# Softmax sums taken once per pair of heads, and two weight operations of VectorE moved to the other half of the pair

## The chip, the cores and the metric

One core of one Trainium2 chip. The metric is the device time of one execution in microseconds (us). The kernel before takes 1670.32 us, the median of 3 runs (1670.14 to 1671.12).

## What is computed

Attention with queries pooled in twos, and behind it a feed-forward layer with tanhshrink:

```python
q_pool = q.reshape(B, H, S // 2, 2, D).mean(axis=3)          # B, H, S, D = 8, 8, 1152, 64
scores = np.matmul(q_pool, k.transpose(0, 1, 3, 2)) / np.sqrt(D)
attn = np.exp(scores - scores.max(-1, keepdims=True))
attn = attn / (attn.sum(-1, keepdims=True) + 1e-09)
x = np.matmul(attn, v)              # to 4608 tokens of 512
h = x @ w_in                        # 512 to 2048
out = (h - np.tanh(h)) @ w_out      # 2048 to 512
```

The product with v is taken with the exponentials as they are. The sums of the exponentials are found beside it, and the division by them comes later, when x is read again.

## The kernel before

**Attention** works on 32 pairs of heads (8 batches of 4 pairs). A pair has 576 pooled queries and 1152 keys, and both heads of a pair lie on the 128 partitions, 64 each. Time is written out by hand in units: a pair has U = 36 units, a half of the queries (HQ = 288) has G = 18, and in every second unit the loop at the end computes one tile of scores of 128 keys (`scores`: eight matmuls, then an exponential of ScalarE into a tile `p_f`). All other work is hung on units by `add(u, f)`, and `run` calls what hangs on a unit, in the order in which it was added. `InOrder` keeps every engine to this order. What the units say is only an order: an engine goes on as soon as the waits of its next instruction are over.

In the same units as the scores of one pair, the next pair is prepared: its operands are split into a high and a low part (`hi_part`, `lo_part`), and the maxima of its scores are found. `max_part` is a matmul of 384 columns for both heads into a double bank of PSUM named `ps`, and in the unit behind it VectorE reduces it into `mx`. There are four double banks in all (`ps_a`), used in turn by scores, maxima, the transpose of the maxima (`turn`) and the products with v. `max_rows`, in the last unit of a first half, makes the maxima of all parts into rows (`nm`, `turn`, `mt`).

At the end of each half (unit 17 of the half) stands `pv`: the product of the nine `p_f` tiles of this half with v, and right behind it `z_sums`, the products of the sums of p with a tile of ones, for the half **before** this one (`late`). The sums over most keys are made by GpSimd (`z_part`: five additions per half into three tiles `z`, of keys 0 to 2, 3 to 5, and 6 and 7); the ninth tile of p goes into the product as it is. In `z_sums` four groups of 32 PSUM partitions are used: heads in steps of 32, tiles in steps of 64, so that each sum comes out in two parts, which `reciprocals` adds.

ScalarE takes both results out of PSUM (`o_out`, `z_out`), the store goes to DRAM once per pair, and once per batch the sums are read back in four DMAs (`sums`), 11 units later VectorE takes the reciprocals (`reciprocals`, two instructions on 128x36), and `spread` writes them for later use.

**Weights** of the feed-forward layer are converted in 32 blocks during attention (`w_block`), one per pair. Offsets count from a unit 5 of a pair. The table of operations gives five operations of VectorE at +48, which is unit 17 of a pair, the end of its first half: clamp, sign, shift, exponent, low part. GpSimd adds at +50 and subtracts at +68, ScalarE converts at +12 and +66.

```python
            for i, op in ((12, begin),
                          (48, lambda: ts(whole(t[0]), whole(t[0]), -top, top, op0=ALU.max, op1=ALU.min)),
                          (48, lambda: ts(t[1], t[0], -0x80000000, None, op0=ALU.bitwise_and)),
                          (48, lambda: stt(t[1], t[0], 3, t[1], op0=ALU.logical_shift_left, op1=ALU.bitwise_or)),
```

**Feed-forward** runs over nine chunks of tokens from line 506 on; its order is set by a scheduler that works from the program.

Of the kernel before, what the change touches and what calls it, by code (L numbers as in the profile page):

```python
# [43 lines left out]
def kernel(  # L44
# [40 lines left out]


    x_dram = dram.tile([NP, P, NTOK], F32, name="x_dram")
    z_dram = dram.tile([B, 2, 2, NP, SQ], F32, name="z_dram")
    r_dram = dram.tile([B, 2, NP, SQ], F32, name="r_dram")
    m_dram = dram.tile([2, 2, 2 * (5 * P + 64)], F32, name="m_dram")  # L90
    wi_dram = dram.tile([NF, P, 2, NP, P], F32, name="wi_dram")
    wo_dram = dram.tile([NF, P, 2, DM], F32, name="wo_dram")
# [1 line left out]
    def load_x(tiles, raw, sp, mul, hi, t0, n):  # L94

        x_h, x_l = (t.rearrange("p (c n) -> p c n", c=NP) for t in tiles())

        t = {}

        def fetch(hp):  # L100
            x, r = t[hp] = raw(hp)
            sp.dma_start(x[:, 0:n], x_dram[hp, :, t0:t0 + n])
            c = t0
            while c < t0 + n:
                b, c1 = divmod(c, SQ)
                m = min(SQ - c1, t0 + n - c)
                for h in range(2):
                    sp.dma_start(r[h * 64:h * 64 + 64, c - t0:c - t0 + m],
                                 r_dram[b, h, hp:hp + 1, c1:c1 + m].broadcast_to([64, m]))
                c += m  # L110

        def divide(hp):
            x, r = t[hp]
            mul.tensor_tensor(x[:, 0:n], x[:, 0:n], r[:, 0:n], op=ALU.mult)  # L114

        def hi_part(hp):
            hi(x_h[:, hp, 0:n], t[hp][0][:, 0:n])

        def lo_part(hp):
            mul.tensor_tensor(x_l[:, hp, 0:n], t[hp][0][:, 0:n], x_h[:, hp, 0:n].bitcast(F32), op=ALU.subtract)  # L120
        return x_h, x_l, [[lambda hp=hp, f=f: f(hp) for f in (fetch, divide, hi_part, lo_part)] for hp in range(NP)]
# [18 lines left out]
    with ExitStack() as actx:  # L140
# [47 lines left out]
        def load(pi):  # L188
            w = pairs[pi] = Pair()
            w.b, w.hp = divmod(pi, NP)  # L190
            w.i = pi % 2
            w.mb = mb[w.i]
            w.q_n = ld.tile([P, 2, SQ], F32, name="q_n")
            w.kq = ld.tile([P, KQ], F32, name="kq")
            sp.dma_start(w.q_n, q[w.b, w.hp])
            sp.dma_start(w.kq[:, SQ:], k[w.b, w.hp])
# [101 lines left out]
        class Half:  # L298
            pass

        late = []

        def z_part(hf, kts):

            z = zp.tile([P, 2, HQ], F32, name="z")
# [5 lines left out]
        def pv(u, hf):  # L311

            w, ps = hf.w, banks()
            hf.o = ps[:, 0]
            for kt in range(KT):
                for h in range(2):
                    pe.matmul(hf.o[64 * h:64 * h + 64, 0:HQ], w.v[:, h, kt], hf.p[kt][:, h], start=(kt == 0),
                              stop=(kt == KT - 1), tile_position=(0, 64 * h))
            add(u + 1, o_out, w, hf, at=first)
            if late:  # L320
                z_sums(u, late.pop(), ps[:, 1])
            late.append(hf)

        def z_sums(u, hf, ps):

            for g, z in enumerate(hf.zs + hf.p[-1:]):
                for h in range(2):
                    r = 64 * (g % 2) + 32 * h
                    pe.matmul(ps[r:r + 32, 0:HQ], ones, z[:, h], start=(g < 2), stop=(g > 1), tile_position=(0, r))
            add(u + 1, z_out, u + 1, hf.w, hf, ps, at=first)  # L330

        def o_out(w, hf):
            if hf.n == 0:
                w.o_s = sm.tile([P, SQ], F32, name="o_s")
                w.z_s = sm.tile([P, SQ], F32, name="z_s")
            act.activation(w.o_s[:, hf.n * HQ:(hf.n + 1) * HQ], hf.o[:, 0:HQ], AF.Copy)

        def z_out(u, w, hf, ps):

            act.activation(w.z_s[:, hf.n * HQ:(hf.n + 1) * HQ], ps[:, 0:HQ], AF.Copy)  # L340
            if hf.n == 1:
                def store():
                    sp.dma_start(x_dram[w.hp, :, w.b * SQ:(w.b + 1) * SQ], w.o_s)
                    sp.dma_start(z_dram[w.b].rearrange("r h a s -> (r h) a s")[:, w.hp], w.z_s[0:P:32])
                add(u + 2, store)
                if w.hp == NP - 1:
                    add(u + 6, lambda: tot.append((w.b, sums(w.b))))
                    if w.b < B - 1:
                        add(u + 17, lambda: reciprocals(dve, *tot[0]))
                        add(u + 20, lambda: spread(sp, *tot.pop(0)))  # L350

        def sums(b):

            n = NP * 2 * SQ // P
            t = rec.tile([P, 2, n], F32, name="rec")
            for r in range(2):
                for h in range(2):
                    sp.dma_start(t[h * 64:h * 64 + 64, r], z_dram[b, r, h].rearrange("a (x n) -> (a x) n", n=n))
            return t

        def reciprocals(eng, b, t):

            eng.scalar_tensor_tensor(t[:, 0], t[:, 0], 1e-9, t[:, 1], op0=ALU.add, op1=ALU.add)
            eng.reciprocal(t[:, 0], t[:, 0])

        def spread(dma, b, t):
            dma.dma_start(r_dram[b].rearrange("h a (x n) -> (h a x) n", n=SQ * NP * 2 // P), t[:, 0])

        WB = 512

        def w_block(u, kind, r, c):

            top = float.fromhex("0x1.dffffep-96")
            raw = wp.tile([P, WB, 2], I32, name="w_raw", bufs=3)
            lo, hi = raw.bitcast(mybir.dt.uint16)[:, :, 1], raw[:, :, 1]
            ts, stt = dve.tensor_scalar, dve.scalar_tensor_tensor
            t = []

            def begin():

                t[:] = [wp.tile([P, WB], I32, name=f"w_{i}", bufs=1 + (i < 2)) for i in range(3)]
                t.append(wp.tile([P, 2, WB], F32R, name="w_hl", bufs=2))
                act.activation(whole(t[0]), whole(hi), AF.Copy, scale=2.0 ** -112)

            def whole(x):
                return x.bitcast(F32)

            def store():
                src = t[3].bitcast(F32)
                if kind == 0:  # L390
                    f = c // P
                    sp.dma_start(wi_dram[f:f + WB // P, :, :, r].rearrange("f p s m -> p s f m"),
                                 src.rearrange("p s (f m) -> p s f m", m=P))
                else:
                    sp.dma_start(wo_dram[r, :, :, c:c + WB], src)
            sp.dma_start(raw.rearrange("p n w -> p (n w)"),
                         (w_in, w_out)[kind][r * P:(r + 1) * P, 2 * c:2 * (c + WB)])
            for i, op in ((12, begin),
                          (48, lambda: ts(whole(t[0]), whole(t[0]), -top, top, op0=ALU.max, op1=ALU.min)),
                          (48, lambda: ts(t[1], t[0], -0x80000000, None, op0=ALU.bitwise_and)),  # L400
                          (48, lambda: stt(t[1], t[0], 3, t[1], op0=ALU.logical_shift_left, op1=ALU.bitwise_or)),
                          (48, lambda: ts(t[2], t[1], -0x800000, None, op0=ALU.bitwise_and)),
                          (48, lambda: stt(whole(t[2]), lo, 2.0 ** -36, whole(t[2]), op0=ALU.mult, op1=ALU.mult)),
                          (50, lambda: pool.tensor_tensor(whole(t[1]), whole(t[1]), whole(t[2]), op=ALU.add)),
                          (66, lambda: act.activation(t[3][:, 0], whole(t[1]), AF.Copy)),
                          (68, lambda: pool.tensor_tensor(t[3][:, 1], whole(t[1]), whole(t[3][:, 0]), op=ALU.subtract)),
                          (75, store)):
                add(u + i, op)
# [63 lines left out]
        for u in range(min(at), 0):  # L472
            run(u, first)
            run(u, early)
            run(u)
        halves = []
        z_groups = {kts[-1]: kts for kts in ((0, 1, 2), (3, 4, 5), (6, 7))}
        for u in range(end + 60):
            run(u, first)
# [2 lines left out]
            if u < end and r % 2 == 0:  # L482
                if r == 0:
                    hf = Half()
                    hf.w, hf.n, hf.p, hf.zs = pairs[n // 2], n % 2, [], []
                    halves.append(hf)
                hf.p.append(pf.tile([P, 2, HQ], F32, name="p_f"))
                scores(hf.w, hf.n, r // 2, hf.p[-1])
                if r // 2 in z_groups:
                    add(u + 1, z_part, hf, z_groups[r // 2])  # L490
            run(u)
            if u < end and r == G - 1:
                pv(u, hf)
            if u == end + 8:
                z_sums(u, late.pop(), banks()[:, 1])
        assert not any(x for t in (at, first, early) for x in t.values())


# [124 lines left out]
```

## Time and profile before

| | us |
|---|---|
| median of 3 runs | 1670.32 |
| lowest, highest | 1670.14, 1671.12 |
| the profiled execution | 1673.38 |
| its span, first to last instruction | 1671.2 |
| TensorE (PE) busy | 1621.1 (97%) |
| VectorE (DVE) busy | 1391.8 (83%) |
| ScalarE (ACT) busy | 1042.8 (62%) |
| GpSimd (POOL) busy | 972.7 (58%) |

The profile is one execution, recorded with every instruction. Attention fills it to about 848 us, and the feed-forward layer the rest. In attention nearly all instructions carry line 37, that of the helper that keeps the order, so they are told apart by their tiles: `ps<-p_f,v` is the product with v, `ps<-z,ones` and `ps<-p_f,ones` are the products of `z_sums`, `ps<-hi` with 384 columns is `max_part`, `mx<-ps` its reduction, `w<-w` an operation on weights, `rec` the reciprocals. A matmul on 4-byte numbers that are not rounded for TensorE shows as two records in a row of the timeline. A row may join several instructions (x2), and its duration then reaches from the first start to the last end.

### The profile page before, as it was taken

How to read it: one execution, taken by the hardware profiler on the slowest of the kernel's cores; microseconds unless marked ns; L12 is line 12 of the kernel's file. 1: busy time of each engine (PE TensorE's matmuls, PEld its weight loads, DVE VectorE, ACT ScalarE, POOL GpSimd, SP SyncE). 2: the span in 40 equal slices, each digit the busy share in tenths (PEclk: the TensorE clock that was granted, in tenths of full speed). 3: DMA queues.
4: the chain of work that ended last, by engine and by line, in shares of the span. 5: the costliest groups of instructions: out<-in, count | busy, mean ns of one | idle time of the engine just before them, and what ended most of it. 6: DMA issues, size and time to landing. Idle time of an engine off the chain costs nothing. (4 is left out here: it accounts for less than half of the span.)

```text
span 1671.2 us, 32291 instructions
## 1 busy us (share of the span) xinstructions
PE 1621.1 (97%) x12640; PEld 1241.3 (74%) x12640; DVE 1391.8 (83%) x1757; ACT 1042.8 (62%) x1961; POOL 972.7 (58%) x696
## 2 busy tenths in 40 slices
PE   6999999999999999999999899999999999999998
PEld 4677667766776677667777678787878788888886
DVE  7887877887878878878659989988898898988897
ACT  3566565655665656556565566666666666666676
POOL 3777877877778778777835625344352626242432
PEclk9999999999999999999999999999999999999999
DMA  3434334333343342434464200102020202010100
GB/s 139 150 115 142 119 111 150 120 114 122 107 152 118 112 150 94 138 121 144 148 236 142 77 28 24 53 14 63 6 71 1 76 1 67 1 51 1 42 14 13
DMA packets 73752, 148.15 MB, mean 89 GB/s; under 512 B 12288, under 2 KB 37504, under 8 KB 73600
## 3 DMA queue, kind: packets, MB, share of 16 engines
q1 hardware_dynamic: 73600, 146.10, 26.7%
q8 instruction: 99, 1.62, 0.4%
q14 instruction: 53, 0.43, 0.1%
HBM read 109.64 MB, written 36.42 MB: 87 GB/s over the span
## 5 line engine op out<-in xcount | busy, mean ns | idle before, releaser
L37 DVE TENSOR_REDUCE mx<-ps 128x2 f32<-128x768 f32 x384 | 360.7, 957 | 142.5 <-PE ps L37 142.4
L536 POOL TENSOR_TENSOR g_lo<-g_s,g_hi 128x512 fp32r<-128x512 f32 (+1 forms) x160 | 208.1, 1301 | 411.0 <-ACT g_hi L535 355.8
L37 ACT ACTIVATE p_f<-ps 128x576 f32<-128x576 f32 x576 | 352.0, 649 | 56.0 <-PE ps L37 41.4
L37 POOL TENSOR_TENSOR z<-p_f 128x576 f32<-128x576 f32 x192 | 279.8, 1457 | 134.5 <-ACT p_f L37 134.5
L518 PE MATMUL ps_h<-x,wi 128*128 128x512 f32 (+1 forms) x1440 | 324.9, 369 | 0.0
L37 PE MATMUL ps<-hi 64*128 64x288 f32 (+1 forms) x1920 | 276.6, 337 | 22.0 <-DVE mx L37 13.5
L37 PE MATMUL ps<-p_f,v 128*64 128x288 f32 x2304 | 293.5, 409 | 0.0
L518 PEld LDWEIGHTS ps_h<-x,wi 128*128 128x128 f32 x1440 | 254.8, 188 | 51.8
L543 PE MATMUL ps_o<-wo,g_hi 128*128 128x512 f32 x1008 | 275.9, 392 | 7.4 <-ACT g_hi L535 7.1
L37 PEld LDWEIGHTS ps<-p_f,v 128*64 128x64 f32 x2304 | 159.8, 137 | 113.2 <-ACT p_f L37 6.8
L37 PEld LDWEIGHTS ps<-hi 64*128 64x128 f32 x1920 | 175.2, 186 | 66.3 <-DVE mx L37 25.5
L543 PEld LDWEIGHTS ps_o<-wo,g_hi 128*128 128x128 f32 x1008 | 186.5, 188 | 50.2 <-ACT g_hi L535 11.3
L37 POOL TENSOR_TENSOR z<-z,p_f 128x576 f32<-128x576 f32 x128 | 184.8, 1444 | 10.0
L535 ACT ACTIVATE g_hi<-g_s 128x512 fp32r<-128x512 f32 (+1 forms) x160 | 94.3, 589 | 151.9 <-DVE g_s L534 150.7
L37 ACT ACTIVATE o_s<-ps 128x288 f32<-128x288 f32 x64 | 26.3, 411 | 254.6 <-PE ps L37 254.6
L531 DVE SCALAR_TENSOR_TENSOR g_w<-g_w,g_u 128x512 f32<-128x512 f32 (+1 forms) x160 | 175.8, 1099 | 0.0
L37 PE MATMUL ps<-hi,lo 64*128 64x288 f32 x1152 | 170.4, 292 | 0.0
L37 PE MATMUL ps<-lo,hi 64*128 64x288 f32 x1152 | 170.4, 292 | 0.0
L37 PE MATMUL ps<-mb,ones_k 64*128 64x288 f32 x1152 | 170.2, 291 | 0.0
L524 ACT ACTIVATE g_u<-ps_h 128x512 f32<-128x512 f32 (+1 forms) x160 | 87.7, 548 | 122.6 <-PE ps_h L518 122.3
L543 PE MATMUL ps_o<-wo,g_lo 128*128 128x512 f32 x504 | 159.7, 392 | 2.9 <-POOL g_lo L536 2.8
L534 DVE COPY_PREDICATED g_s<-g_m,g_t 128x512 f32<-128x512 int32 (+1 forms) x160 | 135.4, 846 | 15.0 <-DVE g_s L533 0.5
(74 smaller groups left out, 2616.9 us busy)
## 6 DMA issues: line engine op xcount, KB each, us to landing
q_n<-in_q_dram SPq DMA_DIRECT2D x32, 576.0 KB
kq<-in_k_dram SPq DMA_DIRECT2D x32, 576.0 KB
v<-in_v_dram SPq DMA_DIRECT2D x32, 576.0 KB
x_dram<-o_s SPq DMA_DIRECT2D x32, 288.0 KB
out_dram<-o_s SPq DMA_DIRECT2D x34, 256.0 KB
w_raw<-in_moe_w_in_dram SPq DMA_DIRECT2D x16, 512.0 KB
wi_dram<-w_hl SPq DMA_DIRECT2D x16, 512.0 KB
w_raw<-in_moe_w_out_dram SPq DMA_DIRECT2D x16, 512.0 KB
```

Source lines behind the costliest of these rows:

```text
L37: ins = self.tc.keep_in_program_order(f(*args, **kwargs))
L518: nc.tensor.matmul(h, wi[fc][:, w, c], x[:, c, 0:n], start=(j == 0), stop=(j == len(mm) - 1))
L524: nc.scalar.activation(u, h, AF.Square)
L531: nc.vector.scalar_tensor_tensor(w, w, PL, u, op0=ALU.mult, op1=ALU.mult)
L534: last = nc.vector.copy_predicated(s1, m.bitcast(I32), th).ins
L535: nc.scalar.activation(g_h, s1, AF.Copy)
L536: nc.gpsimd.tensor_tensor(g_l, s1, g_h.bitcast(F32), op=ALU.subtract)
L543: nc.tensor.matmul(po[j], g[:, ts], wo[fc][:, w], start=(fc == 0 and i == 0), stop=(fc == NF - 1 and i == 2))
```

## The change

`z_sums` is called once per pair, behind the product with v of the second half, for both halves. Each head and half has its own 32 partitions and adds up its four tiles there, so that the sums come out whole; the last tile to be multiplied is the one that GpSimd makes last. ScalarE takes them out once per pair, `sums` is one DMA, and `reciprocals` adds 1e-9 with a `tensor_scalar`. As the sums of a pair now come half a pair earlier, all that hangs on them (store, read-back, reciprocals, spread) moves by 18 units: the reciprocals stand in a unit 17 where they stood in a unit 35. The clamp and the sign of the weights move from +48 to +30, a unit 35, behind `lo_part` of the next pair.

```diff
@@ z_dram, r_dram
-    z_dram = dram.tile([B, 2, 2, NP, SQ], F32, name="z_dram")
-    r_dram = dram.tile([B, 2, NP, SQ], F32, name="r_dram")
+    z_dram = dram.tile([B, NP, 2, SQ], F32, name="z_dram")
+    r_dram = dram.tile([B, NP, 2, SQ], F32, name="r_dram")
@@ pv
             add(u + 1, o_out, w, hf, at=first)
-            if late:
-                z_sums(u, late.pop(), ps[:, 1])
-            late.append(hf)
-
-        def z_sums(u, hf, ps):
-
-            for g, z in enumerate(hf.zs + hf.p[-1:]):
-                for h in range(2):
-                    r = 64 * (g % 2) + 32 * h
-                    pe.matmul(ps[r:r + 32, 0:HQ], ones, z[:, h], start=(g < 2), stop=(g > 1), tile_position=(0, r))
-            add(u + 1, z_out, u + 1, hf.w, hf, ps, at=first)
+            w.halves.append(hf)
+            if hf.n == 1:
+                z_sums(u, w, ps[:, 1])
+
+        def z_sums(u, w, ps):
+
+            parts = [[*hf.zs[:2], hf.p[-1], hf.zs[2]] for hf in w.halves]
+            for g in range(4):
+                for n in range(2):
+                    for h in range(2):
+                        r = 64 * h + 32 * n
+                        pe.matmul(ps[r:r + 32, 0:HQ], ones, parts[n][g][:, h], start=(g == 0), stop=(g == 3), tile_position=(0, r))
+            add(u + 1, z_out, u + 1, w, ps, at=first)
...
-        def z_out(u, w, hf, ps):
+        def z_out(u, w, ps):
 
-            act.activation(w.z_s[:, hf.n * HQ:(hf.n + 1) * HQ], ps[:, 0:HQ], AF.Copy)
-            if hf.n == 1:
...
+            z_s = sm.tile([P, HQ], F32, name="z_s")
+            act.activation(z_s, ps[:, 0:HQ], AF.Copy)
...
+            add(u + 2, store)
+            if w.hp == NP - 1:
+                add(u + 6, lambda: tot.append((w.b, sums(w.b))))
+                if w.b < B - 1:
+                    add(u + 17, lambda: reciprocals(dve, *tot[0]))
+                    add(u + 20, lambda: spread(sp, *tot.pop(0)))
@@ sums, reciprocals
-            t = rec.tile([P, 2, n], F32, name="rec")
-            for r in range(2):
-                for h in range(2):
-                    sp.dma_start(t[h * 64:h * 64 + 64, r], z_dram[b, r, h].rearrange("a (x n) -> (a x) n", n=n))
+            t = rec.tile([P, NP * 2 * SQ // P], F32, name="rec")
+            sp.dma_start(t, by_rows(z_dram[b]))
...
-            eng.scalar_tensor_tensor(t[:, 0], t[:, 0], 1e-9, t[:, 1], op0=ALU.add, op1=ALU.add)
-            eng.reciprocal(t[:, 0], t[:, 0])
+            eng.tensor_scalar(t, t, 1e-9, None, op0=ALU.add)
+            eng.reciprocal(t, t)
@@ w_block
-                          (48, lambda: ts(whole(t[0]), whole(t[0]), -top, top, op0=ALU.max, op1=ALU.min)),
-                          (48, lambda: ts(t[1], t[0], -0x80000000, None, op0=ALU.bitwise_and)),
+                          (30, lambda: ts(whole(t[0]), whole(t[0]), -top, top, op0=ALU.max, op1=ALU.min)),
+                          (30, lambda: ts(t[1], t[0], -0x80000000, None, op0=ALU.bitwise_and)),
...
-            if u == end + 8:
-                z_sums(u, late.pop(), banks()[:, 1])
```

On VectorE, from the end of a second half (`lo`) to the end of the next first half, in a pair behind the last of a batch. Before:

```order
L37 TENSOR_TENSOR lo<-kq,hi 128x1728
L37 SCALAR_TENSOR_TENSOR rec<-rec 128x36
L37 RECIPROCAL rec<-rec 128x36
L37 TENSOR_REDUCE mx<-ps 128x2 x6
L37 TENSOR_REDUCE nm<-mx 128x4 x2
L37 TENSOR_REDUCE nm<-mx_m 128x2
L37 TENSOR_SCALAR w_5047<-w_5047 128x512
L37 TENSOR_SCALAR w_5048<-w_5047 128x512
L37 SCALAR_TENSOR_TENSOR w_5048<-w_5047,w_5048 128x512
L37 TENSOR_SCALAR w_5049<-w_5048 128x512
L37 SCALAR_TENSOR_TENSOR w_5049<-w_raw,w_5049 128x512
L37 TENSOR_REDUCE mx<-ps 128x2
```

The same place with the change:

```order
L37 TENSOR_TENSOR lo<-kq,hi 128x1728
L37 TENSOR_SCALAR w_4659<-w_4659 128x512
L37 TENSOR_SCALAR w_4660<-w_4659 128x512
L37 TENSOR_REDUCE mx<-ps 128x2 x6
L37 TENSOR_REDUCE nm<-mx 128x4 x2
L37 TENSOR_REDUCE nm<-mx_m 128x2
L37 SCALAR_TENSOR_TENSOR w_4660<-w_4659,w_4660 128x512
L37 TENSOR_SCALAR w_4661<-w_4660 128x512
L37 SCALAR_TENSOR_TENSOR w_4661<-w_raw,w_4661 128x512
L37 TENSOR_SCALAR rec<-rec 128x36
L37 RECIPROCAL rec<-rec 128x36
L37 TENSOR_REDUCE mx<-ps 128x2
```

Two operations on weights went up behind `lo`, and the two on `rec`, which stand there once per batch, came down behind the weights, ahead of the reduction `mx` that opens the next half.

On TensorE, at the end of a first half. Before:

```order
L37 MATMUL ps<-hi 128x384 x2
L37 MATMUL ps<-p_f,v 64x288 x18
L37 MATMUL ps<-z,ones 32x288 x6
L37 MATMUL ps<-p_f,ones 32x288 x2
L37 MATMUL ps<-ident,nm 10x128
```

The same place with the change:

```order
L37 MATMUL ps<-hi 128x384 x2
L37 MATMUL ps<-p_f,v 64x288 x18
L37 MATMUL ps<-ident,nm 10x128
L37 MATMUL ps<-hi 128x384 x2
L37 MATMUL ps<-hi 128x288 x2
```

The eight products with ones are gone from there. At the end of the second half sixteen now stand where eight did:

```order
L37 MATMUL ps<-hi,bd_119 128x288 x8
L37 MATMUL ps<-p_f,v 64x288 x18
L37 MATMUL ps<-z,ones 32x288 x8
L37 MATMUL ps<-p_f,ones 32x288 x4
L37 MATMUL ps<-z,ones 32x288 x4
L37 MATMUL ps<-hi 128x384 x2
```

The number of products is the same; in both versions they stand between the product with v and the next `max_part`.

## Rows read from the trace of the kernel before

**Rows 1.** The page: busy time of TensorE, share of the span, instructions.
```profile
PE 1621.1 (97%) x12640; PEld 1241.3 (74%) x12640; DVE 1391.8 (83%) x1757; ACT 1042.8 (62%) x1961; POOL 972.7 (58%) x696
```

**Rows 2.** Waits of TensorE: who waited for whom, us in total, times, longest.
```profile
PE ps L37 <- DVE mx L37: 14.4, 43, 1.2
PE ps_o L543 <- ACT g_hi L535: 8.8, 9, 1.7
```

**Rows 3.** Timeline of TensorE, end of a first half: start, duration (us), [idle before].
```profile
504.55 0.92 PE L37 MATMUL ps<-z,ones 128*32 128x288 f32 x10
505.07 0.41 PE L37 MATMUL ps<-p_f,ones 128*32 128x288 f32 x2
...
505.66 0.27 PE L37 MATMUL ps<-ident,nm 128*10 128x128 f32 x1
505.86 0.57 PE L37 MATMUL ps<-hi 64*128 64x384 f32 x4
...
507.68 0.57 PE L37 MATMUL ps<-hi 64*128 64x384 f32 x4 [0.31 <-DVE mx L37]
```

**Rows 4.** Timeline of VectorE, the same stretch.
```profile
501.51 2.17 DVE L37 TENSOR_SCALAR w<-w 128x512 f32<-128x512 f32 x2
503.72 1.78 DVE L37 SCALAR_TENSOR_TENSOR w<-w,w 128x512 int32<-128x512 int32 x1
505.60 0.43 DVE L37 TENSOR_SCALAR w<-w 128x512 int32<-128x512 int32 x1
506.06 0.69 DVE L37 SCALAR_TENSOR_TENSOR w<-w_raw,w 128x512 f32<-128x512 uint16 x1
506.67 0.95 DVE L37 TENSOR_REDUCE mx<-ps 128x2 f32<-128x768 f32 x1
```

**Rows 5.** Timeline of GpSimd, the same stretch and the next end of a half.
```profile
500.43 1.42 POOL L37 TENSOR_TENSOR z<-p_f 128x576 f32<-128x576 f32 x1
501.92 1.48 POOL L37 TENSOR_TENSOR z<-z,p_f 128x576 f32<-128x576 f32 x1
503.36 1.59 POOL L37 TENSOR_TENSOR z<-p_f 128x576 f32<-128x576 f32 x1
506.83 1.28 POOL L37 TENSOR_TENSOR w<-w,w 128x512 f32<-128x512 f32 x1 [1.89 <-DVE w L37]
...
514.06 1.41 POOL L37 TENSOR_TENSOR z<-p_f 128x576 f32<-128x576 f32 x1
515.42 2.98 POOL L37 TENSOR_TENSOR w_hl<-w,w_hl 128x512 fp32r<-128x512 f32 x1
```

**Rows 6.** Timeline of VectorE, end of the first half of the first pair.
```profile
39.94 0.69 DVE L37 SCALAR_TENSOR_TENSOR w<-w,w 128x512 int32<-128x512 int32 x1
```

**Rows 7.** Timeline of TensorE, end of attention.
```profile
845.58 0.92 PE L37 MATMUL ps<-z,ones 128*32 128x288 f32 x10
...
846.58 0.90 PE L37 MATMUL ps<-z,ones 128*32 128x288 f32 x10
...
848.26 0.50 PE L518 MATMUL ps_h<-x,w 128*128 128x512 f32 x1 [0.53 <-ACT z_s L37]
```

**Rows 8.** Timeline of VectorE, end of a second half, and one reduction 12 us on.
```profile
515.25 2.03 DVE L37 TENSOR_TENSOR lo<-kq,hi 128x1728 fp32r<-128x1728 f32 x1
520.04 0.96 DVE L37 TENSOR_REDUCE mx<-ps 128x2 f32<-128x768 f32 x1 [2.77 <-PE ps L37]
...
532.39 0.95 DVE L37 TENSOR_REDUCE mx<-ps 128x2 f32<-128x768 f32 x1
```

**Rows 9.** Groups by line and shape, VectorE on rec: busy us, mean ns, idle before.
```profile
L37 DVE SCALAR_TENSOR_TENSOR rec<-rec 128x36 f32<-128x36 f32 x7 | 8.8, 1258 | 0.0
L37 DVE RECIPROCAL rec<-rec 128x36 f32<-128x36 f32 x7 | 2.6, 378 | 0.2
L363 DVE SCALAR_TENSOR_TENSOR rec<-rec 128x36 f32<-128x36 f32 x1 | 0.2, 171 | 0.0
```

**Rows 10.** Windows: PE, PEld, DVE, ACT, POOL busy (instructions), PEclk, DMA share, GB/s.
```profile
493.00:499.00 6.00, 6.00 (x88) 5.21 (x82) 3.77 (x4) 4.50 (x9) 2.77 (x2) 1.00 0.82 238
```

More of the change, by code (lines that the diff above doesn't have):

```diff
@@ L108, in fetch @@
                     sp.dma_start(r[h * 64:h * 64 + 64, c - t0:c - t0 + m],
-                                 r_dram[b, h, hp:hp + 1, c1:c1 + m].broadcast_to([64, m]))
+                                 r_dram[b, hp, h:h + 1, c1:c1 + m].broadcast_to([64, m]))
                 c += m
@@ L192, in load @@
             w.mb = mb[w.i]
+            w.halves = []
             w.q_n = ld.tile([P, 2, SQ], F32, name="q_n")
@@ L299 @@
             pass
-        late = []
         def z_part(hf, kts):
@@ L334, in o_out @@
                 w.o_s = sm.tile([P, SQ], F32, name="o_s")
-                w.z_s = sm.tile([P, SQ], F32, name="z_s")
             act.activation(w.o_s[:, hf.n * HQ:(hf.n + 1) * HQ], hf.o[:, 0:HQ], AF.Copy)
-        def z_out(u, w, hf, ps):
-            act.activation(w.z_s[:, hf.n * HQ:(hf.n + 1) * HQ], ps[:, 0:HQ], AF.Copy)
-            if hf.n == 1:
[L342 to L350, printed above, removed]
@@ L352, in sums, with store @@
-        def sums(b):
-            n = NP * 2 * SQ // P
-            t = rec.tile([P, 2, n], F32, name="rec")
-            for r in range(2):
-                for h in range(2):
-                    sp.dma_start(t[h * 64:h * 64 + 64, r], z_dram[b, r, h].rearrange("a (x n) -> (a x) n", n=n))
+        def z_out(u, w, ps):
+            z_s = sm.tile([P, HQ], F32, name="z_s")
+            act.activation(z_s, ps[:, 0:HQ], AF.Copy)
+            def store():
+                sp.dma_start(x_dram[w.hp, :, w.b * SQ:(w.b + 1) * SQ], w.o_s)
+                sp.dma_start(z_dram[w.b, w.hp].rearrange("h (n q) -> (h n) q", q=HQ), z_s[0:P:32])
+            add(u + 2, store)
[4 more added lines that the diff above has]
+                    add(u + 20, lambda: spread(sp, *tot.pop(0)))
@@ L359, in sums, with by_rows @@
+        def by_rows(x):
+            return x.rearrange("a h (x n) -> (a h x) n", n=NP * 2 * SQ // P)
+        def sums(b):
+            t = rec.tile([P, NP * 2 * SQ // P], F32, name="rec")
+            sp.dma_start(t, by_rows(z_dram[b]))
             return t
         def reciprocals(eng, b, t):
-            eng.scalar_tensor_tensor(t[:, 0], t[:, 0], 1e-9, t[:, 1], op0=ALU.add, op1=ALU.add)
-            eng.reciprocal(t[:, 0], t[:, 0])
+            eng.tensor_scalar(t, t, 1e-9, None, op0=ALU.add)
+            eng.reciprocal(t, t)
@@ L366, in spread @@
         def spread(dma, b, t):
-            dma.dma_start(r_dram[b].rearrange("h a (x n) -> (h a x) n", n=SQ * NP * 2 // P), t[:, 0])
+            dma.dma_start(by_rows(r_dram[b]), t)
         WB = 512
@@ L475 @@
             run(u)
-        halves = []
         z_groups = {kts[-1]: kts for kts in ((0, 1, 2), (3, 4, 5), (6, 7))}
@@ L485 @@
                     hf.w, hf.n, hf.p, hf.zs = pairs[n // 2], n % 2, [], []
-                    halves.append(hf)
                 hf.p.append(pf.tile([P, 2, HQ], F32, name="p_f"))
```

## The prediction

> **What bounds the kernel now.** I read the page first: TensorE is busy for 1621.1 of 1671.2 us [rows 1]. Two ways are left to gain time: less work for TensorE, or fewer of the roughly 50 us in which it stands. So the list of its waits comes second. In attention the wait for VectorE's reduction `mx` stands out, with 14.4 us in 43 waits [rows 2]. The window in the middle of attention comes third, as the clock could be the bound instead: TensorE is busy 6.00 of 6.00 us there, at a granted clock of 1.00, its upper level of 2.4 GHz [rows 10]. I leave the clock where it is.
>
> The timeline of TensorE shows where the wait for `mx` lies. At the end of a first half the products with ones begin at 504.55, the transpose at 505.66, the next `max_part` at 505.86, and the one behind it at 507.68 after 0.31 us of idling for `mx` [rows 3]. That idling is one per pair, and 43 waits of 14.4 us are 0.33 each, the same size.
>
> What `mx` was late for stands on VectorE. Behind the maxima it works through five operations on weights: two from 501.51 to 503.68, then three that end at 505.50, 506.03 and 506.75. Only then, at 506.67, does the reduction begin, which ends at 507.62, and TensorE goes on 0.06 later [rows 4]. Its input was there earlier: `max_part` of 505.86 lasted 0.57, to 506.43 [rows 3]. So the weights, not TensorE, set this start. Everything else in the loop is TensorE's own work.
>
> **Why the weight operations look long.** The first of the three lasts 1.78 here, and 0.69 where GpSimd stands idle [rows 6]. Their ends answer to GpSimd's: its `z` end at 501.85, 503.40 and 504.95 [rows 5], and the operations on weights end at 503.68 and 505.50 [rows 4]. If each had waited until about 0.14 before GpSimd's recorded end and had then taken its own 0.43 or 0.69, the ends would be 503.40 − 0.14 + 0.43 = 503.69 and 504.95 − 0.14 + 0.69 = 505.50. Both fit to 0.01. So most of a long row here is a turn of GpSimd, not work. (This reading gives sense to the durations, and everything on the first half below rests on it.)
>
> **The change, part by part.**
>
> *The first half loses the products with ones.* TensorE saves 505.66 − 504.55 = 1.11 us [rows 3]. It is of use only as far as the reduction comes earlier too.
>
> *Two weight operations leave VectorE's chain.* They show 2.17 us [rows 4], but I do not take 2.17. I put the remaining three between GpSimd's turns, starting where the second of VectorE's five could start now: the first in the gap behind GpSimd's first `z`, from 501.85 − 0.14 = 501.71 to 502.40. GpSimd's second `z` follows from some 502.25 with its 1.42, to 503.67. The short operation goes from 503.53 to 503.96, the third `z` from 503.81 to 505.23, the last operation from 505.09 to 505.78. The chain ends at 505.78 where it ended at 506.75: 0.97 earlier, call it 0.98 with the roundings of the starts. One turn of GpSimd fewer stands in the way, and no more.
>
> So the half gets shorter by 0.98, not by 1.11, and the idling behind it grows from 0.31 to about 0.44.
>
> *The second half gets eight products more.* Where two sets stand back to back, the second begins 846.58 − 845.58 = 1.00 behind the first [rows 7]; alone a set cost 1.11, the rest being paid once for the change of tiles. The second half therefore gets longer by 1.00. Nothing there can absorb it, since VectorE's next reduction stands idle for 2.77 waiting for TensorE [rows 8]. The sums it needs are ready: GpSimd's last `z` of a second half ends at 514.06 + 1.41 = 515.47 [rows 5], and the products with ones begin at about 520.04 − 0.57 − 1.11 = 518.36 (the reduction's start, less its `max_part` and a set [rows 3, 8]), 2.9 us later. If that cover were gone, TensorE would stand for it. A pair thus nets 1.00 − 0.98 = 0.02, which the readings do not resolve over some 29 pairs; I take 0. In the three pairs or so without that wait (the first, the last ones) 1.11 is saved against 1.00: −0.3 in all.
>
> *The two operations behind `lo`.* `lo` ends at 515.25 + 2.03 = 517.28, GpSimd's `w_hl` holds until 515.42 + 2.98 = 518.40 [rows 5, 8]. Two more operations of 0.43 each end by about 519.3. The next in the queue is the reduction at 520.04, after 2.77 idle [rows 8], and it moves out by 1.00. Cost 0; without the cover it would be at most 0.9 per pair.
>
> *The reciprocals.* Seven times, once per batch but the last, two operations on `rec` come to stand directly ahead of the critical reduction, behind the weights. They were hidden behind `lo`. The first took 1.26 beside `w_hl` and 0.17 alone, the reciprocal 0.38 [rows 9]. Ahead of it there GpSimd is at the end of its turns, as its addition waits for the last weight operation and starts 0.08 behind it, at 506.83 [rows 4, 5]. So I take the short one: 0.17 + 0.38 and 0.10 between them, 0.65, all of it on the path since TensorE is already idling there. Seven times 0.65 is **+4.5 us**. The bounds are 0 (if the chain no longer ends last) and 1.28 + 0.65, with GpSimd's addition in between [rows 5].
>
> *Feed-forward.* Its first matmul waits 0.53 for `z_s` [rows 7]. `o_s` and `z_s` now come out together behind one burst, so one ScalarE evacuation more stands between: +0.3. The bounds are 0 and the 1.00 of a set.
>
> *The rest.* ScalarE has 32 evacuations fewer, at 62% busy: 0, since TensorE's idling in attention is for VectorE. SP issues one read-back per batch in place of four. It stands behind the stores and weight loads of that unit: at 238 GB/s [rows 10] I estimate their 1.4 MB (by the sizes of the tiles) at 6 us; with units of 25.72 / 36 = 0.71, the stores begin two units behind the end of the products, at about 521, and the read-back lands at about 527. `reciprocals` wants it half a pair later than the chain of this first half, at 505.78 + 25.72 = 531.5, the pair's length being 532.39 − 506.67 [rows 4, 8]. About 4 us of slack cover it; without them every us late costs seven.
>
> **The sum** is −0.3 + 4.5 + 0.3 = +4.5. The profiled execution took 1673.38, 2.2 over its span and 3.1 over the median; I set the sum against the median and get 1670.3 + 4.5 = **1674.8** (1677.9 for an execution under the profiler).
>
> The Trainium skill, "SBUF — State Buffer", section "SBUF: two separate sides", says that certain VectorE operations and any GpSimd operation share a port pair as an exclusive lock, held for the whole instruction by whichever starts first. The ends in rows 4 and 5 agree with it. By that rule the reciprocals' first operation, queued right behind the last weight operation, would start ahead of GpSimd's addition, and the sum would stay +4.5; if the addition were first, the sum would be that of the third rival below. No row shows this order.
>
> **The rivals.**
>
> *The weight operations take all their 2.17 with them (faster).* The mechanism is VectorE's chain: if the three that remain don't inherit the turns of GpSimd, because the `z` shift with them, the chain ends by 506.75 − 2.17 = 504.58. The reduction then waits only for its `max_part`, whose scores come 1.11 earlier, and the idling of 0.31 goes too. The half shortens by 1.42, 0.44 more in each of 29 pairs: −12.8. The reciprocals would fit in front, as 504.58 + 0.65 = 505.23 is before 506.43 − 1.11 = 505.32. That gives 1670.3 − 0.3 + 0.3 − 12.8 = **1657.5**. The point from which it decides: the chain ends before 505.32. A chain between 505.32 and 505.78 gives what lies between. For it speaks that two of five operations leave; against it the ends that fit GpSimd's to 0.01.
>
> *No change.* The reciprocals are covered after all, for instance because the chain no longer ends behind its `max_part` there, and the rest nets nothing: **1670.3**. Against it speaks that it went on 0.06 behind the reduction [rows 3, 4].
>
> *GpSimd's addition takes its turn first.* The reciprocals' first operation then waits 1.28 [rows 5], as the 1.26 against 0.17 shows to be possible [rows 9]. Seven times 1.28 is 9.0: **1683.8**.
>
> *The read-back is late.* It is queued behind more transfers than before. At 2 us late beyond its slack, seven times: +14, **1688.8**. About 4 us of slack speak against it.
>
> **How the numbers follow.** My forecast has 0.48 (its own range is 1671 to 1678, from reciprocals at 0.4 to 1.0 and a pair's net of ±0.02). All of the 2.17 gone, or a good part, has 0.20, no change 0.18, the addition first 0.07, the late read-back 0.07. A measurement of this kernel can tell about 0.2% from no change, 3.3 us: faster is below 1667.0, slower above 1673.7. Of the forecast's 0.48 some two thirds, 0.32, lie above 1673.7 and 0.16 within; with no change that makes 0.34 for the same. The last two add 0.14 to slower, 0.46. Faster is 0.20. The range is 1660 to 1684: it leaves out half of the first rival (0.10) and the late read-back (0.07).
>
> **What would show it.** Right: the stretch of a pair from the end of its first half to the products with v of the second becomes some 0.98 shorter, and the one from there to the next products with v 1.00 longer; TensorE idles about 0.44 ahead of the second `max_part` of a half, and 0.65 more in seven of them; the first weight operation of the three ends within 0.1 of 502.4 on the scale above, the last 0.97 earlier than it did; one run of sixteen products of some 2.1 us. Wrong: that idling gone, so that the halves shorten by 1.42 (first rival); a reciprocal's first operation of over 1 us (third); VectorE idle for a DMA ahead of it (fourth); or TensorE idle between the products with v and those with ones, for `z`.

## The result, and the profile after

| | before | changed |
|---|---|---|
| median, lowest, highest of 5 runs each (us) | 1671.12, 1670.14, 1672.51 | 1677.72, 1676.97, 1679.32 |
| ratio, 95% interval | | 1.0043 [1.0032, 1.0054] |
| first product with v begins at | 36.20 | 39.33 |
| the sixth of the 64 begins at | 102.48 | 106.47 |
| from the sixth to the sixtieth (27 pairs) | 694.67 | 696.88 |
| from there to the feed-forward's first matmul | 51.10 | 51.24 |
| feed-forward, to the end of the span | 822.98 | 820.58 |

The changed kernel is slower by 0.43%; the medians differ by 6.6 us, against the +4.5 that were forecast. The lower rows split each profiled span by the starts of the products with v. They show where the time went: 4.0 us are lost before the sixth of the 64 halves, 2.2 in the 27 pairs behind it, and 0.1 at the end of attention. The feed-forward's 2.4 are dealt with below.

The page and the list of waits, of the changed kernel. They answer to [rows 1, 2]:

```profile
PE 1619.3 (97%) x12640; PEld 1246.5 (74%) x12640; DVE 1410.5 (84%) x1757; ACT 1030.2 (62%) x1929; POOL 969.1 (58%) x696
```

```profile
PE ps L37 <- DVE mx L37: 23.5, 43, 2.6
PE ps_h L515 <- ACT z_s L37: 0.8, 1, 0.8
```

TensorE still waits 43 times for `mx`, but for 23.5 us in place of 14.4, and the longest wait has grown from 1.2 to 2.6.

**A pair in the middle.** TensorE at the end of a first half, then at the end of the second half, with the change (start, duration, [idle before and what ended it]). The first rows answer to [rows 3]:

```profile
508.69 2.35 PE L37 MATMUL ps<-p_f,v 128*64 128x288 f32 x18
510.97 0.27 PE L37 MATMUL ps<-ident,nm 128*10 128x128 f32 x1
511.17 0.57 PE L37 MATMUL ps<-hi 64*128 64x384 f32 x4
...
513.11 0.57 PE L37 MATMUL ps<-hi 64*128 64x384 f32 x4 [0.43 <-DVE mx L37]
...
523.88 1.18 PE L37 MATMUL ps<-z,ones 128*32 128x288 f32 x16
524.88 0.67 PE L37 MATMUL ps<-p_f,ones 128*32 128x288 f32 x8
525.36 0.67 PE L37 MATMUL ps<-z,ones 128*32 128x288 f32 x8
525.96 0.58 PE L37 MATMUL ps<-hi 64*128 64x384 f32 x4
```

The transpose follows on the products with v, the idling of 0.31 has become 0.43, and the joint products take 525.96 − 523.88 = 2.08 us. VectorE in the same stretch answers to [rows 4], GpSimd to [rows 5]:

```profile
507.94 0.87 DVE L37 SCALAR_TENSOR_TENSOR w<-w,w 128x512 int32<-128x512 int32 x1
508.92 1.45 DVE L37 TENSOR_SCALAR w<-w 128x512 int32<-128x512 int32 x1
510.40 1.78 DVE L37 SCALAR_TENSOR_TENSOR w<-w_raw,w 128x512 f32<-128x512 uint16 x1
512.11 0.95 DVE L37 TENSOR_REDUCE mx<-ps 128x2 f32<-128x768 f32 x1
...
526.45 0.96 DVE L37 TENSOR_REDUCE mx<-ps 128x2 f32<-128x768 f32 x1 [1.94 <-PE ps L37]
```

```profile
506.84 1.42 POOL L37 TENSOR_TENSOR z<-p_f 128x576 f32<-128x576 f32 x1
508.34 1.75 POOL L37 TENSOR_TENSOR z<-z,p_f 128x576 f32<-128x576 f32 x1
510.05 1.58 POOL L37 TENSOR_TENSOR z<-p_f 128x576 f32<-128x576 f32 x1
```

The last two of the three operations that stayed last 1.45 and 1.78, where their equals took 0.43 and 0.69 before: they have inherited GpSimd's turns. Their ends fit as before: GpSimd's `z` end at 508.26, 510.09 and 511.63; less 0.14, plus 0.69, 0.43 and 0.69, that gives 508.81, 510.38 and 512.18, and the rows end at 508.81, 510.37 and 512.18. Counted from the start of the product with v (506.45 here, 500.04 before), the first of the three ends at 502.40 and the last at 505.77 on the prediction's scale, which had 502.40 and 505.78.

**The start of the program**, VectorE and then TensorE of the changed kernel, and its windows (PE, PEld, DVE, ACT, POOL busy, PEclk, DMA share, GB/s):

```profile
28.98 1.95 DVE L37 TENSOR_TENSOR lo<-kq,hi 128x1728 fp32r<-128x1728 f32 x1
30.85 1.96 DVE L37 TENSOR_SCALAR w<-w 128x512 f32<-128x512 f32 x2
32.73 1.81 DVE L37 TENSOR_REDUCE mx<-ps 128x2 f32<-128x768 f32 x2
```

```profile
30.82 0.29 PE L37 MATMUL ps<-mb,ones_k 64*128 64x288 f32 x2
33.73 0.40 PE L37 MATMUL ps<-hi 64*128 64x288 f32 x2 [2.62 <-DVE mx L37]
...
35.13 0.44 PE L37 MATMUL ps<-lo,hi 64*128 64x288 f32 x2
```

```profile
32.00:36.00 4.00, 2.27 (x20) 2.27 (x22) 3.41 (x4) 0.65 (x1) 3.35 (x3) 0.76 0.13 50
36.00:40.00 4.00, 4.00 (x46) 3.60 (x44) 2.31 (x4) 3.23 (x6) 3.10 (x3) 0.81 0.00 0
```

Here the two moved operations stand between `lo` and a reduction that TensorE is already waiting for. Before the change that reduction began right behind `lo`, and TensorE idled 0.94 (VectorE, then TensorE of the kernel before):

```profile
30.88 1.82 DVE L37 TENSOR_REDUCE mx<-ps 128x2 f32<-128x768 f32 x2
```

```profile
31.88 0.40 PE L37 MATMUL ps<-hi 64*128 64x288 f32 x2 [0.94 <-DVE mx L37]
```

Now it begins 1.85 later, TensorE idles 2.62, and the granted clock, 1.00 in both windows before, falls to 0.76 and 0.81: a matmul of 288 columns that took 0.29 takes 0.44 for some 3 us. The two operations last 1.96 and not twice 0.43. GpSimd's first `z` begins beside them (GpSimd of the changed kernel):

```profile
30.85 1.67 POOL L37 TENSOR_TENSOR z<-p_f 128x576 f32<-128x576 f32 x1 [21.78 <-ACT p_f L37]
```

It ends at 32.52, and 32.52 − 0.14 + 0.43 = 32.81 is where the row of the two ends. So one turn of GpSimd is in it here too. In the second pair the same two operations of another block stand ahead of a critical reduction, with 2.16 us of idling:

```profile
70.29 1.82 DVE L37 TENSOR_SCALAR w<-w 128x512 f32<-128x512 f32 x2
72.04 0.95 DVE L37 TENSOR_REDUCE mx<-ps 128x2 f32<-128x768 f32 x1
```

**A pair behind the last of a batch**, VectorE, then GpSimd, then TensorE:

```profile
460.29 0.17 DVE L37 TENSOR_SCALAR rec<-rec 128x36 f32<-128x36 f32 x1
460.49 0.38 DVE L37 RECIPROCAL rec<-rec 128x36 f32<-128x36 f32 x1
460.79 0.90 DVE L37 TENSOR_REDUCE mx<-ps 128x2 f32<-128x768 f32 x1
```

```profile
460.44 1.27 POOL L37 TENSOR_TENSOR w<-w,w 128x512 f32<-128x512 f32 x1 [0.63 <-DVE w L37]
```

```profile
461.74 0.44 PE L37 MATMUL ps<-hi 64*128 64x384 f32 x2 [0.88 <-DVE mx L37]
```

The idling is 0.88 there, 0.45 more than in other pairs.

### The profile page after: what moved, and what is told of

Read it like the earlier page. It is cut to its first block, busy times and chain, and to the rows that moved or that the text cites. A ratio compares the mean times of both kernels' runs of the same rounds, so it can differ in the third digit from the quotient of the medians.

```text
span 1675.2 us, 32195 instructions
## 1 busy us (share of the span) xinstructions
PE 1619.3 (97%) x12640; PEld 1246.5 (74%) x12640; DVE 1410.5 (84%) x1757; ACT 1030.2 (62%) x1929; POOL 969.1 (58%) x696
## 4 chain that ended last, share of the span: by engine, by line
PE 60%; DVE 28%; ACT 3%; POOL 3%; issue 3%; DMA 2%; DVEq 0%; POOLq 0%; ACTq 0%; SPq 0%
PE ps L37 35%; PE ps_o L540 13%; PE ps_h L515 12%; DVE w L37 7%; DVE mx L37 6%; DVE g_s L531 3%; DVE g_s L530 3%; DVE g_w L529 3%; DVE g_w L528 2%; DVE g_t L527 2%; DVE g_w L526 1%; DMA x_f<-x_dram 1%; POOL x L120 1%; POOL x_f L114 1%; POOL x L567 1%
## 5 line engine op out<-in xcount | busy, mean ns | idle before, releaser
L37 POOL TENSOR_TENSOR z<-z,p_f 128x576 f32<-128x576 f32 x128 | 192.6, 1505 | 13.5 <-ACT p_f L37 4.1
L528 DVE SCALAR_TENSOR_TENSOR g_w<-g_w,g_u 128x512 f32<-128x512 f32 (+1 forms) x160 | 179.9, 1124 | 0.0
```

Source lines behind the costliest of these rows:

```text
L37: ins = self.tc.keep_in_program_order(f(*args, **kwargs))
L528: nc.vector.scalar_tensor_tensor(w, w, PL, u, op0=ALU.mult, op1=ALU.mult)
```

## The experiments

The theory that these rows give: the loss is that of the start (two weight operations of the first two blocks, ahead of reductions that TensorE waits for) and of the reciprocals, while the joint products and the shorter chain cancel in every other pair. The rivals: the joint products cost something in every pair, or the feed-forward differs. Each time stands beside the kernel before, measured with it on the same chip.

| run | median | before | ratio [95%] |
|---|---|---|---|
| e1, first two blocks as before | 1675.25 | 1671.76 | 1.0021 [1.0012, 1.0030] |
| e2, reciprocals behind lo | 1673.63 | 1671.76 | 1.0012 [1.0004, 1.0021] |
| e3, weights moved alone | 1667.82 | 1671.76 | 0.9972 [0.9961, 0.9982] |
| e4, joint products alone | 1709.02 | 1671.76 | 1.0222 [1.0208, 1.0236] |
| e5, e3 without the first two blocks | 1666.25 | 1672.10 | 0.9966 [0.9953, 0.9978] |
| e6, e1 and e2 together | 1669.30 | 1672.10 | 0.9984 [0.9976, 0.9993] |
| e7, e6 with a third operation moved | 1662.74 | 1672.10 | 0.9942 [0.9928, 0.9955] |
| e8, e7 with one block per pair | 1660.62 | 1670.61 | 0.9940 [0.9926, 0.9953] |
| e9, e5 with one block per pair | 1662.23 | 1670.61 | 0.9947 [0.9934, 0.9959] |
| e8 once more | 1660.91 | 1671.88 | 0.9937 [0.9924, 0.9951] |

**e1, the start.** The offset becomes an argument `o` of `w_block`:

```diff
-                          (30, lambda: ts(whole(t[0]), ...
-                          (30, lambda: ts(t[1], t[0], ...
+                          (o, lambda: ts(whole(t[0]), ...
+                          (o, lambda: ts(t[1], t[0], ...
...
-            add(u, w_block, u, *blk)
+            add(u, w_block, u, 30 if i > 1 else 48, *blk)
```

> The changed kernel, with the clamp and the sign of the first two weight blocks left in their old place. Theory (the start is where most of the loss lies: these operations of two blocks stand ahead of reductions that TensorE waits for while the loop fills): TensorE's longest wait of 2.6 us falls back to about 0.9, the window from 32 to 40 us shows a granted clock of 1.00 again in place of 0.76 and 0.81, the first product with v begins near 36.2 in place of 39.3; the wait of 2.2 us in the second pair goes too, and one behind the second pair grows by up to 0.9. In all about 4 us less than the changed kernel: 1673.7. Rival (the loss lies in every pair, by the joint products): no more than 1 us less, 1677.

The start did as the theory said. The wait at 32 us is 0.98 again, and the clock is back:

```profile
32.00:36.00 4.00, 3.96 (x54) 3.69 (x56) 3.10 (x4) 2.88 (x5) 3.92 (x4) 1.00 0.20 78
36.00:40.00 4.00, 4.00 (x36) 2.36 (x36) 3.93 (x7) 3.61 (x8) 3.69 (x3) 1.00 0.00 0
```

The first product with v begins at 36.37, the wait of 2.16 is 0.42, and one of 1.56 us stands at the end of the second pair, where it was 0.97 before the change and 0.56 with it. The sixth product with v begins at 103.03 in place of 106.47, −3.4; the pairs behind it take 697.03 against 696.88. The median fell by only 2.5, or 3.1 when each is set against its own kernel before (+3.5 in place of +6.6), and the profile's feed-forward was 1.6 longer. The rival's 1677 is out: most of the loss is at the start.

**e2, the reciprocals.**

```diff
-                    add(u + 17, lambda: reciprocals(dve, *tot[0]))
-                    add(u + 20, lambda: spread(sp, *tot.pop(0)))
+                    add(u + 35, lambda: reciprocals(dve, *tot[0]))
+                    add(u + 38, lambda: spread(sp, *tot.pop(0)))
```

> The changed kernel, with the reciprocals 18 units later, behind lo again. Theory (seven pairs idle TensorE for 0.88 us in place of 0.43, which is the reciprocals): the wait is 0.43 in all pairs and the time 7 x 0.45 = 3.2 us less: 1674.5. Rival by the prediction's size of 0.65 each: 4.5 us less, 1673.2. Rival (they are longer behind lo, beside GpSimd, and late there): no gain, 1677.7.

The 27 pairs take 693.86 in place of 696.88, −3.0, and no wait for `mx` among them is over 0.45. The median, 4.1 lower, is nearer to the rival of 0.65 each, but the stretch that the edit touches decides for 0.45; the rest lies outside it (the feed-forward took 819.7 in this profile). Behind `lo` the reciprocals cost nothing, although the first of them takes 1.25 there in place of 0.17 (VectorE, then GpSimd of e2):

```profile
469.28 1.25 DVE L37 TENSOR_SCALAR rec<-rec 128x36 f32<-128x36 f32 x1
...
473.17 0.96 DVE L37 TENSOR_REDUCE mx<-ps 128x2 f32<-128x768 f32 x1 [1.49 <-PE ps L37]
```

```profile
467.49 3.00 POOL L37 TENSOR_TENSOR w_hl<-w,w_hl 128x512 fp32r<-128x512 f32 x1
```

GpSimd's row ends at 470.49, and 470.49 − 0.14 + 0.17 = 470.52, where the row on VectorE ends at 470.53. VectorE still idles 1.49 behind all of it.

**e3 and e4, each half of the change alone.** e3 is the kernel before with 48 turned into 30 for the clamp and the sign; e4 is the changed kernel with 30 turned back into 48.

> The kernel before, with nothing but the clamp and the sign of all weight blocks moved behind lo. Theory (the chain on VectorE ends 0.98 earlier and the reduction then waits for its max_part alone): the wait of 0.31 at the end of a first half goes in some 29 pairs, -9 us, and the start costs its +4: 1666. Rival (the chain of before is not what TensorE waits for there): -0 and +4, 1675.

> The changed kernel, with all operations on weights in their old place, so that the products of the sums are the only part left. Theory (VectorE's chain ends where it did while TensorE is 1.11 us earlier): the wait of 0.31 becomes 1.42, the first half stays 13.9 us less nothing, and the second grows by 1.00: 29 x 1.00 = +29, and +3 from the reciprocals: 1703. Rival (the joint products are free or a gain by themselves, fewer changes of tiles): 1667 to 1674.

e3: the pairs take 687.09 in place of 694.67, −7.6, and the wait of 0.31 is gone from all of them; the sixth product with v begins 3.2 later than before. −9 was a little too much: a pair is shorter by 0.28, not 0.31.

e4: TensorE's wait is 1.42, as worked out, and the pairs take 730.67, +36.0. A pair without reciprocals is 13.88 + 12.79 = 26.67, 0.94 more than before: −0.03 in the first half and +0.97 in the second, so TensorE's gain in the first half was turned wholly into waiting. More than expected came on top, behind the reciprocals. Windows of e4 there:

```profile
367.00:369.00 2.00, 0.38 (x6) 0.15 (x4) 1.93 (x5) 1.22 (x3) 1.05 (x1) 1.00 0.00 0
369.00:371.00 2.00, 1.75 (x22) 1.69 (x24) 1.32 (x3) 0.74 (x2) 1.60 (x2) 0.89 0.31 44
371.00:373.00 2.00, 2.00 (x20) 2.00 (x20) 0.96 (x1) 1.13 (x2) 1.57 (x2) 0.50 0.86 302
373.00:375.00 2.00, 2.00 (x26) 2.00 (x24) 0.99 (x2) 1.33 (x3) 1.92 (x2) 0.75 0.64 263
```

The wait was 1.86 us, and the granted clock fell to 0.50, the lower level of 1.2 GHz, between 1 and 2 us after TensorE went on at 369.25: that half took 15.77 in place of 13.88, 0.45 of it more waiting and the other 1.4 the clock. Of the seven such halves five took 15.8 and two 14.3, where the clock held. Together, 27 × 0.94 + 5 × 1.89 + 2 × 0.44 = 35.7. So the joint products, with the reciprocals that move with them and what the clock costs behind those, are a loss of 2.2% by themselves, and the weights by themselves a gain of 0.3%. What the joint products cost depends on what is left in VectorE's chain.

**e5, e6: is it a matter of adding up?** e5 is e3 with e1's edit, e6 is the changed kernel with the edits of e1 and e2.

> The kernel before, with the clamp and the sign moved behind lo for all weight blocks but the first two. Theory (the start's loss of 4 us is the first two blocks', and the gain of moving them elsewhere stays): 7.6 us less than before between the third pair and the thirtieth, and a start within 0.5 of before's: 1663.5 to 1664.5. Rival (the start's loss stays, as block 0 meets block 3's operations at one place): 1667.5.

> The changed kernel with both losses mended: the first two blocks in their old place and the reciprocals behind lo. Theory (losses add up, and the joint products are worth nothing by themselves as long as three operations stay in VectorE's chain): 1677.7 - 3.4 - 3.0, 1671 to 1672, no change from before. Rival (joint products gain once they are freed of the two losses): 1667 or less.

e5 came out between its two cases. The first product with v begins at 36.19 again, but at the end of the second pair block 0's five operations meet block 3's two behind one `lo`; TensorE idles 2.84 us, that half takes 16.36, where it took 12.98 before and a steady one takes 11.82, and the sixth product with v begins 1.9 later than before, where e3 was 3.2 late.

e6 fell 2.8 below before, where none was expected. Up to the feed-forward its profile is 847.9 us long, that of before 848.3: attention is the same to 0.4, as the theory has it. What was faster in this profile is the feed-forward, 818.2 against 823.0: TensorE's waits for `g_hi` and `g_lo`, which stand there, sum to 10.7 us against 15.4. A part of its 0.16% therefore lies where the edits do nothing that these runs explain.

**e7, the shift moved too**, on top of e6:

```diff
-                          (48, lambda: stt(t[1], t[0], 3, t[1], ...
+                          (o, lambda: stt(t[1], t[0], 3, t[1], ...
```

> As the run with both losses mended, with the shift moved behind lo as well, so that two operations on weights stay at the end of the first half. Theory (those two end at GpSimd's second turn, before max_part; TensorE waits for nothing there): the wait of 0.43 goes in some 27 pairs, -11.6 us against that run, 1660, and so 3 us less than moving two weight operations alone does. Rival (the shift is late behind lo, or its cost returns through GpSimd's turns): 1671.

With two operations left at the end of the first half, VectorE is early, and TensorE waits for nothing (VectorE, then TensorE of e7):

```profile
500.16 0.62 DVE L37 TENSOR_SCALAR w<-w 128x512 int32<-128x512 int32 x1
500.81 1.78 DVE L37 SCALAR_TENSOR_TENSOR w<-w_raw,w 128x512 f32<-128x512 uint16 x1
503.88 0.96 DVE L37 TENSOR_REDUCE mx<-ps 128x2 f32<-128x768 f32 x1 [1.29 <-PE ps L37]
```

```profile
503.20 0.28 PE L37 MATMUL ps<-ident,nm 128*10 128x128 f32 x1
503.40 0.57 PE L37 MATMUL ps<-hi 64*128 64x384 f32 x4
...
504.90 0.62 PE L37 MATMUL ps<-hi 64*128 64x384 f32 x4
```

The pairs take 683.83, 9.9 less than e6's 693.68 (expected 11.6: a half is 0.37 shorter, not 0.43). At the end of the second pair eight operations of two blocks stand behind one `lo`, with 3.68 us of idling and the granted clock at 0.50 for 6 us behind it: that half takes 19.22, 6.4 more than a steady one and 4.7 more than in e6, and the sixth product with v begins 3.0 later than e6's. The median is 6.6 below e6's, where 11.6 was expected; the 1.7 that the pairs lack and the 3.0 of the start make nearly all of the difference.

```profile
84.00:86.00 2.00, 0.00 (x0) 0.00 (x0) 2.00 (x3) 0.00 (x0) 0.58 (x1) 0.80 0.99 313
86.00:88.00 2.00, 1.94 (x16) 1.95 (x18) 0.87 (x2) 0.52 (x1) 0.00 (x0) 0.50 1.01 322
88.00:90.00 2.00, 2.00 (x20) 2.00 (x18) 0.96 (x1) 1.06 (x3) 1.72 (x2) 0.50 0.42 127
90.00:92.00 2.00, 2.00 (x20) 2.00 (x18) 0.96 (x1) 1.06 (x3) 2.00 (x2) 0.50 0.00 0
```

**e8 and e9, one block per pair**, on top of e7 and of e5:

```diff
-            u = U * (i - 2) + 5 if i else 23
-            add(u, w_block, u, 30 if i > 1 else 48, *blk)
+            u = U * (i - 1) + 5
+            add(u, w_block, u, 30 if i else 48, *blk)
```

> As the run with three operations moved, with the blocks of weights one pair later each, one per pair, so that no two blocks meet in the second pair (the last block falls into the last pair, where VectorE has no maxima to find). Theory (eight operations of two blocks behind one lo idle TensorE for 3.7 us there, and its clock falls behind that, 6.4 us in all): that half has the length of the others, 12.8 in place of 19.2, and the time is 6.4 us less: 1656. Rival (the last block delays the end of attention or the feed-forward's weights): 1662.

> As the run of the kernel before with two operations moved save in the first two blocks, with the blocks one pair later each. Theory: the half of 16.4 becomes one of 11.8, 4.5 us less, 1661.7, and against the joint products, where no run has a wait left in the pairs, the sums per half cost 25.45 - 25.32 = 0.13 in each of some 30 pairs, 4 us, with what the feed-forward differs by on top. Rival (one burst for both halves is worth nothing by itself): the same as the joint products within 1 us.

Both lost the long half (it takes 12.78 and 11.82), and no wait for `mx` in the pairs is over 0.25 us in either. e9 came out as expected; its rival, a time within 1 us of the joint products', is not decided by medians that differ by 1.3 to 1.6. e8 is 4.6 above its 1656, although its 27 pairs take 683.50 against e9's 687.25, the expected 0.13 each. Its profile lost time elsewhere: its first product with v begins at 38.41, and its feed-forward takes 824.75, the longest of all. So it was run once more:

> The run with three operations moved and one block per pair, once more. Its first profile began the products with v at 38.4 us in place of 36.1 and took 824.8 in the feed-forward, where all others took 818 to 823. Theory (chance of one execution): 36.1 and 818 to 823 here, a median of 1657 to 1659. Rival (the order of this kernel): both again, 1660.6.

Both came again, at 37.83 and 823.27. That speaks for the order of this kernel and does not show it. What the 2 us of the start are, the traces say: in both profiles of e8 a matmul of 288 columns takes 0.44 us up to about 36 us, where it takes 0.29 from 30.1 on in e9, while the granted clock of the windows reads 1.00 in both kernels. The profile of e4 has the same long stretch (its first product with v begins at 37.77), so it is not e8's alone, and what sets it stays open. So does the length of the feed-forward: e9 has the last block at the same place, and its feed-forward took 820.95. By the medians e7, e8 and e9 can't be told apart, since their intervals overlap; all are faster than the kernel before by 0.5 to 0.6%.

**The feed-forward's 2.4 us.** Two runs of the unchanged programs, for a second profile each:

> The changed kernel as it is, for a second profile. The feed-forward took 820.6 us in its first profile. Theory (its length differs from execution to execution of one program): outside 820.1 to 821.1. Rival (it belongs to the order of its instructions): within.

> The kernel before as it is, for a second profile. The feed-forward took 823.0 us in its first profile. Theory (its length differs from execution to execution): it differs by over 0.5, so that the 2.4 us between the two versions are no effect of the change. Rival: within 0.5 of 823.0.

The changed kernel took 821.2 there, 0.1 outside the stated band, and the kernel before 820.8, after 823.0 in its first profile. The 2.2 between the two lie in TensorE's waits for `g_hi` and `g_lo`: 15.4 us in the first profile, 13.3 in the second. The length of this part differs by 2 us between two executions of one program, so the 2.4 between the versions are no effect that these runs show.

## Why the prediction was right or wrong

By the steps of the prediction:

- **The chain ends 0.98 earlier: right.** A first half is 12.92 in place of 13.91, −0.99, and the idling behind it 0.43, as forecast (0.44). The reading that a long row on VectorE is mostly a turn of GpSimd's fits the changed kernel's ends to 0.01. The first rival let the whole 2.17 leave the chain, and no idling would have remained. e7 shows where its condition does hold: with two operations left, not three.
- **The second half gets 1.00 longer: right**, 12.79 against 11.82, +0.97. The last `z` is ready 3 us ahead, since GpSimd's last one ends at 520.78 and the products begin at 523.88.
- **A pair nets nothing: right.** 25.71 against 25.73. e4 shows how much hung on it: without the weights' move it is +0.94.
- **The two operations behind `lo` cost 0: this is the step that failed.** It holds in the middle, where VectorE still idles 1.94 behind them. It was read from one pair at 520 us and taken for all 32. In the first pair the reduction behind `lo` began right at its end, so there was no cover, and it came 1.85 later: 0.86 of work and a turn of GpSimd, which the prediction's bound of 0.9 without the cover leaves out. A fall of the clock came on top (+3.1 by the first product with v). In the second pair block 0's two stand ahead of the reduction that closes a first half. Together +4.0; e1 takes back 3.4 of them. The waits of [rows 2] were read as one per pair of 0.33 each. Twelve of the 43 are short ones of 0.16 to 0.27 ahead of 27 us, and the three longest, 0.94, 0.97 and 1.21, end at 31.88, 82.96 and 96.22: the list held the start, and the timeline of TensorE there would have shown it.
- **The reciprocals: right in place, too large in size.** 0.45 each, not 0.65; 7 × 0.45 = 3.2, and e2 measures 3.0. The first of them took 0.17 and not 1.28: it began at 460.29, ahead of GpSimd's addition at 460.44, so the third rival is out. That the same operation can wait e2 shows, with 1.25 beside `w_hl`. What was counted too much is the 0.10 between them, 0.03 in the rows, and the overlap of recorded ends: the reduction begins at 460.79, while the reciprocal is recorded to 460.49 + 0.38 = 460.87. The Trainium skill, "SBUF — State Buffer", section "SBUF: two separate sides", has the shared ports go to whichever starts first; the 0.17 in all seven places agrees.
- **The feed-forward's start, +0.3: right**, 0.53 has become 0.83. With the −0.3 taken for the pairs without a wait, the end of attention should come out about even; it is 0.14 longer.
- **The read-back has slack: right.** No idle time stands ahead of the first operation on `rec`.
- **The rest of the pairs:** of the +2.2, the reciprocals make 3.2; the kernel before had one wait of 0.66 in place of 0.31 in a late pair, which is gone (−0.35), and 27 times −0.02 is another −0.5.

The sum of the forecast was thus made of right mechanisms for the steady pairs, +3.2 where 4.5 stood, and lacked the start's 4.0. Attention is 6.3 us longer in the profile, the medians differ by 6.6. That 1677.7 lies within the forecast's own 1671 to 1678 is partly luck: the places that the sum names changed by 2.2 + 0.1 = 2.3 us, which would have counted as no change, and the rest is the start, which stood at 0.

## What to carry to other kernels

A move that is free in a steady loop has to be looked up in the loop's first passes too, where the same wait may have no slack, as here in the first two pairs: list each place at which the moved instruction is issued, and read the idle time of the engine ahead of it at each. Where two engines take turns, as VectorE and GpSimd do here, count the turns that remain ahead of the critical instruction, not the durations in the rows that leave. And a part that saves the bound engine's time (here the joint products, which gain 0.13 a pair at best) is worth nothing until the other engine's chain is shortened by more than that.

## What the runs showed that was not expected

A wait of some 2 us can cost TensorE twice. After 1.86 us of idling in e4 the granted clock fell (five times of seven) to 0.50, and a matmul of 288 columns took 0.45 in place of 0.29 for some 3 us; after 1.42 us in the pairs beside it it stayed at 1.00. But the length of the idling alone doesn't decide. The wait in the second pair was 2.16 and 2.15 in two executions of the changed kernel: in the first the clock stayed at 1.00, in the second it fell, and so it did in e2 after 2.17 (windows of the second):

```profile
72.00:74.00 2.00, 1.04 (x14) 1.04 (x16) 1.65 (x4) 0.03 (x1) 1.29 (x1) 1.00 0.02 3
74.00:76.00 2.00, 2.00 (x22) 1.90 (x20) 1.37 (x2) 1.33 (x3) 1.23 (x1) 0.59 0.72 172
76.00:78.00 2.00, 2.00 (x22) 2.00 (x20) 0.89 (x1) 1.13 (x2) 1.58 (x2) 0.56 0.98 402
```

That half took 16.10 in place of 14.63, and the one behind it 12.79 in place of 13.52, as a wait of 0.56 there was gone; the sixth product with v began at 106.37 and 106.47. And the feed-forward, with the same instructions in the same order, took 823.0 and 820.8 us in two executions of the kernel before, which is as much as several of the effects above. Whether the chip plays a part these two do not separate, but beside e1 to e4 the 24 executions of that kernel on one chip already lie between 1670.39 and 1673.59.
